# Matmuls of zeros ahead of the first load, of the coarse scores and of the local transposes

## The chip, the cores and the metric

The kernel runs on one core of one Trainium2 chip. The metric is device time in microseconds (us) of one execution. The median of 3 runs of the kernel before is 862.72 us (860.76 to 865.24).

## What is computed

Attention on q, k, v of shape (4, 8, 576, 64) in float32, and two gated layers on its output. The attention has two parts that are added: a coarse one on means of 4 neighbours, repeated 4 times, and a local one in which each position sees the positions less than 4 away.

```python
q_d, k_d, v_d = (x.reshape(B, H, S // 4, 4, D).mean(axis=3) for x in (q, k, v))
out_up = np.repeat(sm_attn(q_d, k_d, v_d), 4, axis=2)
mask = np.abs(pos[:, None] - pos[None, :]) < 4
scores = np.where(mask, scale * q @ k.T, -1e9)
out_local = softmax(scores) @ v
x = (out_up + out_local)           # to 2304 tokens x 512
x = max(x @ w1, x @ w2, x @ w3) @ w_out
out = ((x @ w_a) * (x @ w_b)) @ w_out2
```

## The kernel before

The work has three stages. The attention runs over 16 items, each a batch and a pair of heads. The first layer follows in six blocks of 384 tokens, and the second layer in products that TensorE runs almost without a gap. The matrices of both layers are split into a high and a low part, and every product is three matmuls. The weights come in as 8-byte numbers and are converted on VectorE in four steps (`convert_steps`, lines 519 to 536: `ce`, `cm`), then split by ScalarE (line 541) and GpSimd (line 542).

An item goes through six steps. `a_load_qk` and `a_load_v` (letters k and v) issue its loads on SP's queue: q, k, the coarse v (`vr`, line 230) and the windows of v (`vw`, line 254). `a_qk` (Q) transposes q and k on TensorE for the first eight items (`ps_t`, lines 291 and 296), copies them out on ScalarE (`kt`, `qt`) and sums them on VectorE to coarse ones (`kd`, `qp`, scaled into `qd`). `a_scores` (S) runs the coarse scores (`ps_sd`, line 322), the mask (`ps_s`, line 327: a bf16 matmul of 320 columns) and the local scores (line 340), and the two softmaxes: maxima `md` and `ml`, exponentials `ed` and `el`, sums, and on GpSimd the division of `ed` (line 383) and of `el` (line 390). `a_tr` (T) adds up the coarse v on GpSimd (`vr`, line 401, in place; `vd`, line 402) and transposes `ed` (`ps_td`, line 412) and `el` (`ps_tl`, line 423). `a_av` (A) runs the weighted sums (`ps_ud`, line 438; `ps_av`, line 460), adds them on VectorE (`x`, line 470) and splits the result (`xh` on ScalarE, `xl` on GpSimd, line 484).

The strings `PRE` and `LOOPS` say in which order the steps of several items are written: at item i the loads are two or three items ahead, the transposes of q and k two ahead, and the scores one ahead. From item 4 on, pieces of the first layer (`ps_m`, line 654) are mixed in at a lower priority. Within the attention the engines' orders aren't those of the text: a scheduler puts instructions in order by a timeline of its own, so an added instruction can move others on every engine. At run time each engine and each queue keeps its order and waits at the head of it. After the attention the order is that of the text (`manual_schedule`).

PSUM gives the attention eight banks: `bk("t")` and `bk("v")` take three in turn, and all other names five in turn. The items below 8 with an odd number share one `vr` tile, and all the others share another, so a new `vr` load waits until GpSimd has read the old one (`vd`).

Of the kernel before, what the change touches and what calls it, by code (L numbers as in the profile page):

```python
# [10 lines left out]
BF16 = mybir.dt.bfloat16  # L11
# [34 lines left out]
SUM_ACT = (0, 1, 2, 3, 4, 6, 7, 8, 9, 10, 13, 14, 15)  # L46
NORM_POOL = (0, 1, 2, 3, 4, 5, 6, 7, 8, 9, 10, 11, 13, 14, 15)
ADD_PSUM = range(16)


@with_exitstack
def attn_moe_kernel(
# [14 lines left out]
    nc = tc.nc  # L67
# [4 lines left out]
    P = 128  # L72
# [4 lines left out]
    TB = 384  # L77
# [5 lines left out]
    RF = S // P  # L83
    RT = S - RF * P
# [12 lines left out]
    def win(t):  # L97
        return t * QT - (FAC - 1)

    def clip(t):  # L100
        return max(win(t), 0), min(win(t) + KW, S)

    def nq(t):
        return min(QT, S - t * QT)
# [12 lines left out]
    def bk(st, name):  # L117
        if 1 in psp_:
            return psp_[1].tile([P, 512], F32, tag="m", name=name)
        t, n = ("t", 3) if st in "tv" else ("m", 5)  # L120
        return psp_[0].tile([P, 512], F32, tag=t, name=name, bufs=n)
# [3 lines left out]
    ap_ = attn_ctx.enter_context(tc.tile_pool(name="attn", bufs=1, side="right"))  # L125
# [4 lines left out]
    def at(v):  # L130

        return tc.high_priority(offset=tc.cur_priority - int(v))

    ident = cst.tile([P, P], F32, name="ident")
    make_identity(nc, ident)
# [48 lines left out]
    def pool(i, n):  # L184

        return ex if i < NI // 2 and i % n == n - 1 else ap_
# [9 lines left out]
    TV = NI // 2  # L196
# [114 lines left out]
    def half_of(j, t):  # L311

        return 1 - j if t >= NP2 else j
# [3 lines left out]
    def a_scores(i):  # L317
        s = st[i]
        psd = bk("s", "ps_sd")
        pd = psd[: 2 * DQ, : NDQ * SD].rearrange("m (t k) -> m t k", t=NDQ)  # L320
        for t in range(NDQ):
            nc.tensor.matmul(  # L322
                pd[:, t, :], s["qd"][:, t].rearrange("m j i -> m (j i)"), s["kd"], start=True, stop=True
            )
        psl = [bk("s", "ps_s") for _ in GS]
        for (g0, g1), ps in zip(GS, psl):
            nc.tensor.matmul(
                ps[:, : (g1 - g0) * KW],
                identb,
                cap[:, g0:g1, :].rearrange("m t k -> m (t k)"),  # L330
                start=True,
                stop=True,
            )
        for j, t in order_s:
            half = half_of(j, t)
            g = int(t >= GS[1][0])
            pj = slice(64 * j, 64 * j + 64)
            k0, k1 = clip(t)
            o = (t - GS[g][0]) * KW - win(t)
            nc.tensor.matmul(  # L340
                psl[g][64 * half : 64 * half + nq(t), o + k0 : o + k1],
                s["qt"][pj, t * QT : t * QT + nq(t)],
                s["kt"][pj, k0:k1],
                start=False,
                stop=True,
                skip_group_check=True,
            )
        ed = s["ed"] = pool(i, 3).tile([2 * DQ, NDQ, SD], F32, tag="ed", bufs=1 if pool(i, 3) is ex else 2, name="ed")
        el = s["el"] = pool(i, 3).tile([P, NQ, KW], F32, tag="el", bufs=1 if pool(i, 3) is ex else 2, name="el")
        md = pool(i, 3).tile([2 * DQ, NDQ, 1], F32, tag="md", bufs=1 if pool(i, 3) is ex else 2, name="md")  # L350
        sd = pool(i, 3).tile([2 * DQ, NDQ, 1], F32, tag="sd", bufs=1 if pool(i, 3) is ex else 2, name="sd")
        ml = pool(i, 3).tile([P, NQ, 1], F32, tag="ml", bufs=1 if pool(i, 3) is ex else 2, name="ml")
        sums = epss[i % 3]
        sl = pool(i, 3).tile([P, NQ, 1], F32, tag="sl", bufs=1 if pool(i, 3) is ex else 2, name="sl")
        if i in SUM_ACT:
            nc.vector.tensor_reduce(out=md[:, :, 0], in_=pd, axis=AX.X, op=ALU.max, negate=True)
            for t in range(NDQ):
                nc.scalar.activation(
                    out=ed[:, t, :],
                    in_=pd[:, t, :],  # L360
                    func=AF.Exp,
                    bias=md[:, t, :],
                    accum_out=sums[: 2 * DQ, NQ + t, :1],
                )
        else:
            nc.vector.tensor_reduce(out=md[:, :, 0], in_=pd, axis=AX.X, op=ALU.max)
            nc.vector.tensor_tensor(out=ed, in0=pd, in1=md.to_broadcast([2 * DQ, NDQ, SD]), op=ALU.subtract)
            nc.scalar.activation(out=ed, in_=ed, func=AF.Exp)
        for (g0, g1), ps in zip(GS, psl):
            e = el[:, int(g0 > 0) :: 2, :]  # L370
            n = g1 - g0
            p3 = ps[:, : n * KW].rearrange("m (t k) -> m t k", t=n)
            nc.vector.tensor_reduce(out=ml[:, g0:g1, 0], in_=p3, axis=AX.X, op=ALU.max)
            nc.vector.tensor_tensor(
                out=e, in0=p3, in1=ml[:, g0:g1, :].to_broadcast([P, n, KW]), op=ALU.subtract
            )
            nc.scalar.activation(out=e, in_=e, func=AF.Exp, scale=SCALE)
        if i not in SUM_ACT:
            nc.vector.tensor_reduce(out=sums[: 2 * DQ, NQ:, 0], in_=ed, axis=AX.X, op=ALU.add)
        nc.vector.tensor_reduce(out=sd[:, :, 0], in_=sums[: 2 * DQ, NQ:], axis=AX.X, op=ALU.add)  # L380
        nc.vector.reciprocal(sd, sd)
        eng = nc.gpsimd if i in NORM_POOL else nc.vector
        eng.tensor_tensor(out=ed, in0=ed, in1=sd.to_broadcast([2 * DQ, NDQ, SD]), op=ALU.mult)
        for g0, g1 in GS:
            e = el[:, int(g0 > 0) :: 2, :]
            n = g1 - g0
            nc.vector.tensor_reduce(out=sums[:, g0:g1, 0], in_=e, axis=AX.X, op=ALU.add)
            nc.vector.tensor_reduce(out=sl[:, g0:g1, 0], in_=sums[:, g0:g1], axis=AX.X, op=ALU.add)
            nc.vector.reciprocal(sl[:, g0:g1], sl[:, g0:g1])
            nc.gpsimd.tensor_tensor(  # L390
                out=e, in0=e, in1=sl[:, g0:g1, :].to_broadcast([P, n, KW]), op=ALU.mult
            )
# [4 lines left out]
    def a_tr(i):  # L397
        s = st[i]
        s["vd"] = ap_.tile([DK, NDK, 2, D], F32, tag="vd", bufs=2, name="vd")
        vr = s["vr"].rearrange("p h c f d -> p (h c) f d")  # L400
        nc.gpsimd.tensor_tensor(out=vr[:, :, 0:2, :], in0=vr[:, :, 0:2, :], in1=vr[:, :, 2:4, :], op=ALU.add)  # L401
        nc.gpsimd.tensor_tensor(
            out=s["vd"].rearrange("p c h d -> p h c d"),
            in0=s["vr"][:, :, :, 0, :],
            in1=s["vr"][:, :, :, 1, :],
            op=ALU.add,
        )
        ptd = s["ptd"] = pool(i, 2).tile([DK, NDK, NDQ * 2 * DQ], F32, tag="ptd", bufs=1, name="ptd")
        for c in range(NDK):
            ps = bk("t", "ps_td")  # L410
            for t in range(NDQ):
                nc.tensor.transpose(
                    ps[:DK, t * 2 * DQ : (t + 1) * 2 * DQ],
                    s["ed"][:, t, c * DK : (c + 1) * DK],
                    ident[: 2 * DQ, : 2 * DQ],
                )
            nc.scalar.copy(ptd[:, c, :], ps[:DK, : NDQ * 2 * DQ])
        pt = s["pt"] = []
        for u0 in range(0, NP2, TG):
            ps = bk("t", "ps_tl")  # L420
            n = min(TG, NP2 - u0)
            for u in range(n):
                nc.tensor.transpose(  # L423
                    ps[:, u * P : (u + 1) * P],
                    s["el"][:, 2 * (u0 + u) : 2 * (u0 + u) + 2, :].rearrange("m a x -> m (a x)"),
                    ident,
                )
            x = pool(i, 2).tile([P, TG, P], F32, tag="pt", bufs=3, name="pt")
            nc.scalar.copy(x[:, :n].rearrange("m t k -> m (t k)"), ps[:, : n * P])
            pt.append(x)  # L430

    def a_av(i):
# [34 lines left out]
        for (g0, g1), ps in zip(AVG, pss):  # L467
            a0, a1 = g0 * QT, min(g1 * QT, S)
            if i in ADD_PSUM:
                mark['d', i] = nc.vector.tensor_tensor(  # L470
# [5 lines left out]
            else:  # L476
                nc.scalar.copy(x32[:, a0:a1], ps[:, : a1 - a0])
        if i not in ADD_PSUM:
            xg = x32.rearrange("m (g f) -> m g f", f=FH)
# [582 lines left out]
    for x in PRE.split():  # L1062
        if x == "w":
            w_prefetch()
        elif x == "s":
            with at(tc.cur_priority + 0):
                w_step(1)
        else:
            emit(x[0], int(x[1:]))
# [208 lines left out]
```

## Time and profile before

| | us |
|---|---|
| Median of 3 runs | 862.72 |
| The profiled execution, its own time | 866.62 |
| Its span, first to last instruction | 864.8 |
| TensorE (PE) busy | 831.2 |
| VectorE (DVE) busy | 625.9 |
| GpSimd (POOL) busy | 368.8 |
| ScalarE (ACT) busy | 336.3 |

The span is the time that the trace shows; 1.8 us of the execution lie outside it. PE's busy time is that of its matmuls, whose ends are modelled, and it doesn't tell a matmul at 2.4 GHz from one at 1.2 GHz; the granted clock of a stretch (1.00 or 0.50 of full speed) does. The profiled execution is 3.9 us (0.45%) slower than the median.

### The profile page before, as it was taken

What the parts mean: (1) busy time and instruction counts of PE and PEld (TensorE: products, weight loads), DVE (VectorE), ACT (ScalarE), POOL (GpSimd) and SP (SyncE); (2) the same over time, 40 slices, a digit from 0 to 9 for tenths busy, and PEclk for the clock granted to TensorE, in tenths of its full rate; (3) what the DMA queues carried; (4) which work ended last, traced back from release to release, by engine and by line L of the source; (5) the groups of instructions that cost most, each with busy time, mean ns of one, the idle gap of its engine ahead of it and who ended that gap; (6) DMA issues with size and microseconds to landing.
All of it is one profiled execution on the core that took longest, in us unless ns stands there. A gap on an engine that the chain in (4) does not pass through costs nothing.

```text
span 864.8 us, 14914 instructions
## 1 busy us (share of the span) xinstructions
PE 831.2 (96%) x5686; PEld 771.1 (89%) x5686; DVE 625.9 (72%) x1110; ACT 336.3 (39%) x755; POOL 368.8 (43%) x354
## 2 busy tenths in 40 slices
PE   5988989999999999999989999999999999999998
PEld 3667778899999999999988999999999799999997
DVE  5989987765664795696788899999999754234344
ACT  4775645543321231332435553443444332322211
POOL 3865775442322241334546654645554341111111
PEclk9799899999999999999999999999999999999999
DMA  8896764411220130231324454544453268666612
GB/s 182 181 180 140 146 122 96 78 29 31 72 73 25 51 96 25 90 142 73 110 98 147 171 185 156 183 181 161 181 183 134 99 223 303 231 216 219 243 49 74
DMA packets 125553, 116.32 MB, mean 135 GB/s; under 512 B 81834, under 2 KB 108202, under 8 KB 125482
## 3 DMA queue, kind: packets, MB, share of 16 engines
q1 hardware_dynamic: 121306, 98.59, 38.3%
q10 hardware_dynamic: 4176, 16.78, 5.5%
q8 instruction: 45, 0.74, 0.4%
q14 instruction: 26, 0.21, 0.1%
HBM read 80.74 MB, written 34.60 MB: 133 GB/s over the span
## 4 chain that ended last, share of the span: by engine, by line
PE 74%; DVE 10%; DMA 6%; POOL 5%; issue 3%; ACT 1%; SPq 1%; DVEq 0%; POOLq 0%; ACTq 0%
PE ps_m L654 45%; PE ps_u L911 23%; DMA vr<-in_v_dram 4%; PE ps_av L460 1%; DVE ce L519 1%; POOL el L390 1%; PE ps_tl L423 1%; POOL vr L401 1%; DVE ce L529 1%; PE ps_ud L438 1%; DVE g L940 1%; PE ps_sd L322 1%; DMA w<-y 1%; DVE cm L522 1%; PE ps_s L340 1%
## 5 line engine op out<-in xcount | busy, mean ns | idle before, releaser
L654 PE MATMUL ps_m<-xh,w 128*128 128x384 f32 x864 | 174.5, 340 | 0.3 <-ACT xh L483 0.3
L950 POOL TENSOR_TENSOR gl<-g,gh 128x384 fp32r<-128x384 f32 x72 | 78.0, 1083 | 185.6 <-ACT gh L949 156.2
L654 PEld LDWEIGHTS ps_m<-xh,w 128*128 128x128 f32 x864 | 152.4, 190 | 2.3 <-issue 0.8
L911 PE MATMUL ps_u<-xh,w 128*128 128x384 f32 x720 | 135.9, 338 | 0.1
L911 PEld LDWEIGHTS ps_u<-xh,w 128*128 128x128 f32 x720 | 128.1, 190 | 2.7 <-DVE t L683 0.4
L654 PE MATMUL ps_m<-wo,gh 128*128 128x512 f32 (+1 forms) x422 | 126.9, 393 | 1.5 <-DVE acc L1019 1.3
L911 PE MATMUL ps_u<-xl,w 128*128 128x384 f32 x648 | 122.2, 336 | 1.6 <-ACT sn L923 1.6
L911 PEld LDWEIGHTS ps_u<-xl,w 128*128 128x128 f32 x648 | 113.7, 188 | 5.0 <-ACT sn L923 2.5
L654 PE MATMUL ps_m<-xl,w 128*128 128x384 f32 x432 | 94.3, 336 | 1.7 <-POOL xl L484 1.7
L923 ACT COPY sn<-ps_u 128x384 f32<-128x384 f32 x108 | 50.6, 479 | 113.2 <-PE ps_u L911 99.4
L683 DVE TENSOR_TENSOR t<-ps_m,t 128x384 f32<-128x384 f32 x72 | 39.9, 554 | 72.7 <-PE ps_m L654 65.2
L654 PEld LDWEIGHTS ps_m<-wo,gh 128*128 128x128 f32 x422 | 78.0, 188 | 15.4 <-DVE acc L1019 3.0
L1019 DVE TENSOR_TENSOR acc<-ps_m,acc 128x512 f32<-128x512 f32 (+1 forms) x91 | 61.2, 679 | 41.6 <-PE ps_m L654 41.6
L654 PEld LDWEIGHTS ps_m<-xl,w 128*128 128x128 f32 x432 | 76.3, 188 | 2.1 <-POOL xl L484 1.9
L654 PE MATMUL ps_m<-hh,wo 128*128 128x384 f32 x288 | 74.0, 336 | 2.4 <-DVE acc L710 2.4
L689 POOL TENSOR_TENSOR hl<-t,hh 128x384 fp32r<-128x384 f32 x36 | 37.0, 1026 | 69.3 <-ACT hh L688 68.2
L654 PE MATMUL ps_m<-wo,gl 128*128 128x512 f32 x211 | 66.2, 392 | 0.0
L949 ACT CAST gh<-g 128x384 fp32r<-128x384 f32 x72 | 37.1, 515 | 71.4 <-DVE g L940 67.7
L710 DVE TENSOR_TENSOR acc<-ps_m,acc 128x384 f32<-128x384 f32 x120 | 61.7, 552 | 0.6 <-PE ps_m L654 0.5
L526 ACT ACTIVATE ce<-ce,ebias 128x512 int16<-128x512 uint16 x60 | 43.3, 722 | 45.4 <-DVE ce L519 45.3
L842 POOL TENSOR_TENSOR w<-F,w 128x768 fp32r<-128x768 f32 (+1 forms) x36 | 56.6, 1589 | 5.2 <-ACT w L840 4.6
L527 DVE SCALAR_TENSOR_TENSOR cm<-raw,cm 128x512 f32<-128x512 uint32 x60 | 56.3, 938 | 1.5
(131 smaller groups left out, 1334.7 us busy)
## 6 DMA issues: line engine op xcount, KB each, us to landing
dw<-w SPq DMA_DIRECT2D x24, 768.0 KB
raw<-in_moe_w_dram SPq DMA_DIRECT2D x18, 512.0 KB
raw<-in_moe_w_out_dram SPq DMA_DIRECT2D x18, 512.0 KB
w<-dw SPq DMA_DIRECT2D x12, 768.0 KB
w<-dw ACTq DMA_DIRECT2D x12, 768.0 KB
dw<-wo SPq DMA_DIRECT2D x12, 512.0 KB
wo<-dw ACTq DMA_DIRECT2D x11, 512.0 KB
vw<-in_v_dram SPq DMA_DIRECT2D x62, 80.0 KB
```

The source lines that it names most:

```text
L526: nc.scalar.activation(out=s16, in_=e, func=AF.Relu, bias=ebias, scale=8.0)
L527: nc.vector.scalar_tensor_tensor(out=f, in0=lo, scalar=2.0**-32, in1=m, op0=ALU.mult, op1=ALU.add)
L654: nc.tensor.matmul(ps, lhs[a], rhs[b], start=(i == 0), stop=(i == n - 1))
L683: nc.vector.tensor_tensor(out=t, in0=ps, in1=cur["t"], op=ALU.max)
L689: nc.gpsimd.tensor_tensor(out=l, in0=t, in1=h.bitcast(F32), op=ALU.subtract)
L710: nc.vector.tensor_tensor(out=a, in0=ps, in1=a, op=ALU.add)
L842: nc.gpsimd.tensor_tensor(out=l, in0=w, in1=h.bitcast(F32), op=ALU.subtract)
L911: nc.tensor.matmul(ps, w[:, a, slot, kk], y[:, b * HK + kk], start=start and i == 0, stop=i == 3 * HK - 1, skip_group_check=not start,)
L923: nc.scalar.copy(t, ps)
L949: nc.scalar.copy(h, g)
L950: nc.gpsimd.tensor_tensor(out=l, in0=g, in1=h.bitcast(F32), op=ALU.subtract)
L1019: nc.vector.tensor_tensor(out=a, in0=ps, in1=a, op=ALU.add)
```

## The change

A tile `idle` of zeros, 128 x 384 in bf16, is written once by VectorE. A helper `warm` runs a given number of matmuls of it into a PSUM bank: 128 x 128 zeros as weights, 384 columns. Nothing reads the results. It stands in three places: 14 matmuls ahead of everything that TensorE does; for items 0 to 8 in the bank of the coarse scores ahead of these scores (9, 9, 4, 4, 4, 4, 4, 4, 3), for items 0 to 7 behind one more transpose of the tail of q; and for items 0 to 9 in the bank of the local transposes ahead of these (8, 4, 4, 4, 4, 4, 4, 4, 6, 6). That is 14 + 45 + 48 = 107 matmuls, each with its load of weights, and 8 transposes.

```diff
+WARM_FIRST = 14
+WARM_S = (9, 9, 4, 4, 4, 4, 4, 4, 3)
+WARM_T = (8, 4, 4, 4, 4, 4, 4, 4, 6, 6)
...
+    idle = ap_.tile([P, TB], BF16, name="idle")
+    nc.vector.memset(idle, 0.0)
+
+    def warm(ps, n):
+
+        for _ in range(n):
+            nc.tensor.matmul(ps[:, :TB], idle[:, :P], idle, start=True, stop=True)
+
+    warm(bk("q", "ps_w"), WARM_FIRST)
+
     ident = cst.tile([P, P], F32, name="ident")
...
         psd = bk("s", "ps_sd")
+        if i < len(WARM_S):
+            if i < TV:
+                nc.tensor.transpose(psd[:, :RT], s["q"][:RT, RF], ident[:RT, :RT])
+            warm(psd, WARM_S[i])
         pd = psd[: 2 * DQ, : NDQ * SD].rearrange("m (t k) -> m t k", t=NDQ)
...
             ps = bk("t", "ps_tl")
+            if u0 == 0 and i < len(WARM_T):
+                warm(ps, WARM_T[i])
             n = min(TG, NP2 - u0)
```

Line numbers behind the added code grow by 4 to 20. On GpSimd, between the setup and the third weight piece, this stood before (`ed` of items 0 and 1, `el` of items 0 and 1, the coarse v of item 1, then 0, then 2 and 3):

```order
L383 TENSOR_TENSOR ed<-ed,sd 96x432
L401 TENSOR_TENSOR vr<-vr 72x4x128
L542 TENSOR_TENSOR w_141<-cm,w_140 128x512
L390 TENSOR_TENSOR el<-el,sl 128x5x64
L401 TENSOR_TENSOR vr<-vr 72x4x128
L390 TENSOR_TENSOR el<-el,sl 128x5x64
L402 TENSOR_TENSOR vd<-vr 72x2x2x64 x2
L383 TENSOR_TENSOR ed<-ed,sd 96x432
L542 TENSOR_TENSOR w_141<-cm,w_140 128x512
L390 TENSOR_TENSOR el<-el,sl 128x5x64 x2
```

On the same engine, from the same place on, this stands there now:

```order
L419 TENSOR_TENSOR vr<-vr 72x4x128
L401 TENSOR_TENSOR ed<-ed,sd 96x432
L562 TENSOR_TENSOR w_158<-cm,w_157 128x512
L408 TENSOR_TENSOR el<-el,sl 128x5x64 x2
L419 TENSOR_TENSOR vr<-vr 72x4x128
L420 TENSOR_TENSOR vd<-vr 72x2x2x64 x2
L562 TENSOR_TENSOR w_158<-cm,w_157 128x512
L401 TENSOR_TENSOR ed<-ed,sd 96x432
L408 TENSOR_TENSOR el<-el,sl 128x5x64
L419 TENSOR_TENSOR vr<-vr 72x4x128
L504 TENSOR_TENSOR xl<-x_446,xh 128x384
L504 TENSOR_TENSOR xl<-x_446,xh 128x192
```

Both halves of item 0's `el` (line 390, now 408) have moved ahead of the second wait for a `vr` load, and the second half of item 1's `el`, which stood ahead of `xl` and of the `vr` of items 2 and 3, now comes behind them (it is the next row but two).

On SP's queue, between the `vr` load of item 7 and that of item 8 (the first and the last row), this stood before:

```order
L230 DMA vr<-in_v_dram 72x4x256
L254 DMA vw<-in_v_dram 64x5x64 x4
L505 DMA raw<-in_moe_w_dram 128x4x256
L210 DMA k<-in_k_dram 32x18x32 x4
L210 DMA q<-in_q_dram 32x18x32
L254 DMA vw<-in_v_dram 64x5x64 x4
L210 DMA q<-in_q_dram 32x18x32 x3
L230 DMA vr<-in_v_dram 72x4x256
```

And this stands on SP's queue now, from the `vr` load of item 7 on:

```order
L244 DMA vr<-in_v_dram 72x4x256
L525 DMA raw<-in_moe_w_dram 128x4x256
L224 DMA q<-in_q_dram 32x18x32 x4
L244 DMA vr<-in_v_dram 72x4x256
L268 DMA vw<-in_v_dram 64x5x64 x4
L525 DMA raw<-in_moe_w_out_dram 128x1024
L224 DMA k<-in_k_dram 32x18x32 x4
```

Between the `vr` loads of items 7 and 8 stood 17 issues, and now 5 stand there.

On PE, ahead of the last of item 9's weighted sums, 133 matmuls of the first layer (`ps_m`) stood before, and 130 stand there now.

## Rows read from the trace of the kernel before

**Rows 1.** Busy time by stretch: us, engines' busy us (instructions), PE clock, DMA share, GB/s

```profile
0.00:131.30 131.30, 108.63 (x1334) 87.36 (x1335) 111.20 (x257) 78.40 (x236) 86.38 (x109) 0.88 0.77 156
131.30:864.80 733.50, 722.61 (x4353) 683.71 (x4353) 514.72 (x853) 257.85 (x519) 282.44 (x246) 1.00 0.38 131
```

**Rows 2.** Waits of PE, 0 to 131.3 us: us in total, times, longest

```profile
PE ps_tl L423 <- POOL el L390: 8.4, 5, 3.1
PE ps_t L291 <- DMA k<-in_k_dram: 3.9, 1, 3.9
PE ps_sd L322 <- ACT qd L265: 3.5, 2, 1.8
```

**Rows 3.** PE alone in seven stretches: busy us (x), clock, DMA share, GB/s

```profile
3.86:14.20 10.34, 7.55 (x65) 1.00 0.84 193
...
28.17:34.98 6.81, 6.81 (x66) 0.51 0.76 185
...
sum 41.03, PE 36.07; mean PE 5.15
```

**Rows 4.** Timeline of PE: start, us, operation, count, idle before and its releaser

```profile
3.86 1.09 PE L291 MATMUL ps_t<-ident,k 128*128 128x128 f32 x4 [3.86 <-DMA k<-in_k_dram]
...
10.78 0.74 PE L327 MATMUL ps_s<-cap,identb 128*128 128x320 bf16 x2
...
16.54 0.60 PE L291 MATMUL ps_t<-ident,k 128*128 128x128 f32 x4
...
22.62 0.47 PE L327 MATMUL ps_s<-cap,identb 128*128 128x320 bf16 x1
...
65.47 0.43 PE L327 MATMUL ps_s<-cap,identb 128*128 128x320 bf16 x2
```

**Rows 5.** Waits of DVE, 0 to 131.3 us

```profile
DVE qp L302 <- PE ps_t L291: 6.7, 3, 4.9
DVE md L356 <- PE ps_sd L322: 2.7, 2, 2.3
```

**Rows 6.** All engines, 20 to 120 us; then 67.64 to 71.14 us

```profile
20.00:120.00 100.00, 86.48 (x1106) 68.79 (x1107) 94.74 (x218) 65.48 (x202) 71.26 (x76) 0.86 0.77 157
...
67.64:71.14 3.50, 2.73 (x24) 2.14 (x18) 3.50 (x3) 2.09 (x9) 3.50 (x6) 1.00 0.67 147
```

**Rows 7.** Line 527 in 20 to 120 us (busy, mean ns); then all (min/median/max ns)

```profile
L527 DVE SCALAR_TENSOR_TENSOR cm<-raw,cm 128x512 f32<-128x512 uint32 x7 | 10.2, 1456 | 0.0
...
L527 DVE SCALAR_TENSOR_TENSOR cm<-raw,cm x60: 641/693/3503, 13.6 to 670.5; 128x512 f32<-128x512 uint32 x60
```

**Rows 8.** Timeline of POOL, and its wait for `vr` to 131.3 us

```profile
26.05 1.17 POOL L390 TENSOR_TENSOR el<-el,sl 128x320 f32<-128x320 f32 x1
27.18 1.86 POOL L402 TENSOR_TENSOR vd<-vr 72x256 f32<-72x256 f32 x2
...
31.65 1.40 POOL L390 TENSOR_TENSOR el<-el,sl 128x320 f32<-128x320 f32 x2
...
35.73 2.93 POOL L401 TENSOR_TENSOR vr<-vr 72x512 f32<-72x512 f32 x2
...
74.19 0.72 POOL L402 TENSOR_TENSOR vd<-vr 72x256 f32<-72x256 f32 x1
...
86.00 1.27 POOL L401 TENSOR_TENSOR vr<-vr 72x512 f32<-72x512 f32 x1 [6.15 <-DMA vr<-in_v_dram]
...
POOL vr L401 <- DMA vr<-in_v_dram: 24.7, 9, 6.2
```

**Rows 9.** Timeline of SP's queue: issue of `vr` of items 2 and 3, and of 8

```profile
30.52 0.88 SPq L230 DMA_DIRECT2D vr<-in_v_dram  x2
...
82.29 0.41 SPq L230 DMA_DIRECT2D vr<-in_v_dram  x1
```

**Rows 10.** Timeline of PE: local transposes of items 0 and 1

```profile
27.27 0.76 PE L423 MATMUL ps_tl<-ident,el 128*128 128x128 f32 x5 [1.86 <-POOL el L390]
...
36.95 0.55 PE L423 MATMUL ps_tl<-ident,el 128*128 128x128 f32 x3
```

## The prediction

> **What bounds the kernel now.** I read the busy time by stretch first, because the change touches ten items at the front alone. Up to 131.3 us, where item 9's weighted sums end, PE is busy 108.6 us and idle 22.7; behind that point it is busy 722.6 of 733.5 us [rows 1]. So what is behind 131.3 us is bound by PE and stays as it is, and a lead or a lag at that point is handed on almost whole. How much of the first layer is mixed in by then hardly changes either, as the order stands: 133 of its matmuls before, 130 now.
>
> Ahead of that point I read who waits. PE waits 8.4 us for GpSimd's `el` ahead of the local transposes, 3.9 us for the first load, and 3.5 us for ScalarE's `qd` ahead of the coarse scores [rows 2]. These are the places where the zeros stand. Then the clock: six stretches granted near half speed, and the first one, whose record says 1.00 but whose transposes take 1.09 us for four against 0.60 later, hold 36.1 us of PE's work [rows 3, 4]. The falls come behind waits of PE, as the stretch that begins at 28.17 us comes behind the wait of 1.86 us that ended at 27.27 [rows 3, 10].
>
> Last, the other engines. VectorE is busy 94.7 us of the 100 between 20 and 120 us [rows 6], more than PE. GpSimd waits 24.7 us for the loads of `vr`, and what stands behind such a wait in its order is late with it [rows 8].
>
> **What is added, and its price.** The nearest row to an idle matmul is the mask's: bf16, 128 x 128 weights, 320 columns. At half clock two of them take 0.74 us and one 0.47, so one follows another in 0.27; at full clock the two take 0.43 [rows 4]. By columns (384 to 320) an idle matmul costs 0.32 us at 1.2 GHz, and I take half of that, 0.16, at 2.4 GHz; both are estimates. The 107 cost 17.2 us at full clock and 34.2 at half. The first 14 will be at half, which adds 2.2. The eight transposes are narrower than those of k at 0.60 us for four, so they cost 1.2 us at most, and I take that. The one memset on VectorE, and the loads of weights beside the matmuls, I cost at nothing: at its place VectorE waits for PE, the longest time 4.9 us [rows 5], and if that cover were gone the memset would cost no more than some tenths, by `vd`'s 0.72 us for a longer operation on GpSimd [rows 8].
>
> **What the clock gives back.** If no stretch falls to half speed, 36.1 us of work become 18.0. So PE's own account to 131.3 us is 108.6 + 17.2 + 2.2 + 1.2 - 18.0 = 111.2 us, 2.6 more than now. The zeros cost what the clock returns. A gain can come only out of the 22.7 us in which PE is idle: 131.3 - 111.2 = 20.1 us is the bound on that side. On the other side, if the clock stays low, 93 matmuls ahead of scores and transposes cost 30.0 us, of which the waits of 8.4 and 3.5 us take 11.9: 18 us slower. Between these ends the chain of waits decides, so I walk it.
>
> **The start.** The 14 matmuls wait for the memset alone. No row shows how early VectorE can run it; with 1 us as an estimate and 4.5 for the matmuls, they end 1.6 us behind the first load's 3.86 [rows 4]. Against that, transposes at full clock save 0.5 us for each four. I take 0 here, with 1.6 lost and 1.0 gained as its ends.
>
> **Item 0.** Both halves of its `el` now stand ahead of GpSimd's second wait for `vr`; the second half ended at 27.2 us [rows 8], and PE's local transposes followed at 27.27 [rows 10]. Its `vd` moves up by that half, 1.2 us, and the half-speed transposes of k behind it lose another 0.5. With the smaller shares of the sums I take 2.0 us gained.
>
> **Item 1.** Here the new order is worse. Its `el` ran at 31.65 us; its second half now stands behind the `vr` of items 2 and 3, which were issued at 30.52 [rows 9] and read from 35.73 to 38.66, behind one `vd` and two `xl` [rows 8]. At 0.9 us for each of these three that half ends at about 35.7 + 2.9 + 2.8 + 0.7 = 42.1 us, and the transposes at 36.95 [rows 10] come some 5 us later. SP's queue repays this: the load of item 8's `vr` could have been issued when `vd` of item 6 ended at 74.9, and was issued at 82.29, behind 17 others; GpSimd waited 6.15 us for it at 86.0, with item 6's `el` behind [rows 8, 9]. With 5 between, up to 6 us of that go. The load of item 5 moves up in the same way. What is late next is VectorE.
>
> **The limit.** VectorE has 5.3 us idle between 20 and 120 us [rows 6]. A faster PE can take these, not its work. I take 4 of the 5.3. That gives 2.0 + 4.0 = 6.0 us at 131.3, handed to the end.
>
> VectorE's busy time isn't all work, though. Line 527 takes 1.46 us on average between 20 and 120 us and 0.64 at best, and 3.50 at worst, from 67.64 us on [rows 7]; in just these 3.50 us GpSimd is busy all the time [rows 6]. For its seven runs alone that is 7 x 0.82 = 5.7 us of waiting that depends on how GpSimd's work falls. In the new order it can shrink or grow, which is why I don't go to the end of the 5.3.
>
> The Trainium skill (SBUF — State Buffer, "Who interferes with whom") says that a VectorE instruction with two SBUF inputs and a GpSimd instruction that reads SBUF exclude each other, the loser blocked for the whole of the other. The trace agrees with it at 67.64 us. By that rule a GpSimd whose waits shrink gives VectorE fewer openings, so the conversions would get no shorter and the gain would end at item 0's 2.0 us: the first rival below.
>
> **Sum.** 866.6 us for the profiled execution becomes 860.6. It was 3.9 us above the median, so the median goes from 862.7 to 856.7. What a measurement tells from no change here is about 0.5%, 4.3 us: faster is below 858.4, slower above 867.0.
>
> **Rivals.**
>
> *VectorE holds the pace* (18%). The zeros run inside waits that end when they ended before, and VectorE's conversions wait for GpSimd as they do now. For it speaks 94.7 us busy of 100; against it, that VectorE waits 6.7 and 2.7 us for PE at transposes and coarse scores [rows 5]. Only part of item 0 is gained, the 5 us of item 1 are repaid and no more: 861 to 864 us. The rule of the Trainium skill (SBUF — State Buffer, "Who interferes with whom") points to this case.
>
> *Item 1's `el` is not repaid* (14%). GpSimd stands at the `vr` of items 2 and 3, PE waits 5 us ahead of item 1's transposes, and all later items are that much late; the clock falls in that wait, and a stretch such as the one of 6.81 us at half speed, all of it work [rows 3], loses 3.4 more. With 2.0 gained at item 0 that is 5 + 3.4 - 2.0 = 6.4 us: 869. It decides from the point where less than 1 us of the 5 comes back through SP's earlier loads.
>
> *Everything gives way* (18%). VectorE's waits beside GpSimd shrink with the new order by half or more of the 5.7 us of line 527 and of the like in the other conversion steps, and PE's idle time goes from 22.7 to under 12. Then 9 to 16 us are gained: 847 to 854.
>
> That the zeros don't raise the clock is part of the second rival; that they are hidden and raise it is common to the other cases.
>
> **How the numbers follow.** The forecast has 50%, its own range 853.7 to 860.7 (2 to 9 us gained). About three quarters of it lie below 858.4: 0.37 and the 0.18 of the last rival make 0.55 for faster. The rest of it and the first rival make 0.30 for no change, and the second 0.15 for slower with a margin. The range to hold 8 of 10 runs from 847, the far end of the largest gain, to 867, where the slower case begins.
>
> **What would show it.** The granted clock should be 1.00 from some 6 us on, with one or no stretch at half speed to 131 us. Idle matmuls should take 0.16 us each. PE's wait for `el` ahead of item 0's transposes should be gone, the one ahead of item 1's should be new and of 3 to 5 us. GpSimd's 6.15 us wait at 86 should shrink below 2. VectorE between 20 and 120 us should stay above 94 us busy. Item 9's sums should end near 125 us, and the rest should take 733 us as now. The prediction is wrong if that rest changes by over 3 us, if VectorE's busy time up to item 9 falls by over 6 us, or if PE's idle time there, with the zeros counted as work, stays above 18.

## The result and the profile after

The changed kernel takes 874.32 us (median of 6 runs, 870.14 to 878.54); the kernel before took 862.55 beside it (6 runs). The ratio is 1.012, 95% interval 1.0081 to 1.0158: slower by 11.8 us, where 6.0 us faster was forecast, and above the range that was given. The profiled execution took 878.54 us with a span of 876.2; it is 4.2 us above its median, as the one before was 3.9 above its own.

Busy time by stretch comes first, cut where item 9's weighted sums end (142.41 us now, 131.3 in [rows 1]), then the stretch of [rows 6] and the two longest at half clock; the columns are those of [rows 1].

```profile
0.00:142.41 142.41, 125.35 (x1444) 94.52 (x1445) 109.32 (x257) 79.44 (x235) 84.98 (x109) 0.88 0.71 144
142.41:876.25 733.84, 722.75 (x4358) 684.54 (x4358) 515.61 (x854) 257.80 (x520) 282.01 (x245) 1.00 0.38 130
20.00:120.00 100.00, 87.27 (x1084) 65.71 (x1084) 86.59 (x199) 60.11 (x180) 65.07 (x69) 0.86 0.71 149
41.00:51.00 10.00, 10.00 (x113) 7.09 (x113) 7.97 (x19) 4.66 (x17) 5.25 (x6) 0.51 0.63 163
78.00:92.00 14.00, 13.64 (x116) 9.15 (x116) 12.02 (x20) 6.83 (x19) 8.90 (x9) 0.51 0.51 109
```

The whole loss is ahead of that cut: 11.1 us of it, and behind it 733.84 us stand against 733.50. PE is busy 16.7 us longer and idle 17.1 us in place of 22.7. The granted clock is 0.88, as before: the zeros did not keep it up. VectorE is busy 86.6 us of 100 in place of 94.7 [rows 6], so it is further from full than it was.

The waits of PE to 142.41 us, and those of GpSimd, answer to [rows 2] and [rows 8]: us in total, times, longest.

```profile
PE ps_tl L443 <- POOL el L408: 7.2, 3, 3.9
PE ps_td L430 <- POOL ed L401: 2.7, 1, 2.7
PE ps_ud L458 <- POOL vd L420: 2.2, 1, 2.2
...
POOL vr L419 <- DMA vr<-in_v_dram: 33.7, 8, 11.9
POOL el L408 <- DVE sl L407: 6.3, 4, 3.4
```

The waits ahead of the first load and of `qd` are gone, as they should be: zeros run there now. But PE now waits 2.7 us for item 5's `ed` and 2.2 us for `vd`, both of GpSimd, and GpSimd stands 33.7 us at `vr`, 9 more than before (11.9 of them ahead of the first `vr`, which now comes ahead of item 0's `ed`). Where that is, the timelines of GpSimd and PE show.

```profile
34.77 1.27 POOL L419 TENSOR_TENSOR vr<-vr 72x512 f32<-72x512 f32 x1 [2.32 <-DMA vr<-in_v_dram]
...
39.86 0.90 POOL L408 TENSOR_TENSOR el<-el,sl 128x320 f32<-128x320 f32 x1
...
74.27 1.26 POOL L419 TENSOR_TENSOR vr<-vr 72x512 f32<-72x512 f32 x1 [5.62 <-DMA vr<-in_v_dram]
...
77.41 0.90 POOL L401 TENSOR_TENSOR ed<-ed,sd 96x432 f32<-96x432 f32 x1
78.27 1.39 POOL L408 TENSOR_TENSOR el<-el,sl 128x320 f32<-128x320 f32 x2
```

```profile
24.98 0.77 PE L443 MATMUL ps_tl<-ident,el 128*128 128x128 f32 x5 [0.26 <-POOL el L408]
27.95 0.72 PE L458 MATMUL ps_ud<-ptd,vd 72*64 72x144 f32 x8 [2.20 <-POOL vd L420]
...
40.82 1.32 PE L443 MATMUL ps_tl<-ident,el 128*128 128x128 f32 x5 [3.94 <-POOL el L408]
44.69 1.46 PE L144 MATMUL ps_sd<-idle 128*128 128x384 bf16 x4
...
78.36 0.70 PE L430 MATMUL ps_td<-ident,ed 96*72 96x96 f32 x3 [2.66 <-POOL ed L401]
...
80.90 1.46 PE L144 MATMUL ps_tl<-idle 128*128 128x384 bf16 x4
...
90.98 1.13 PE L480 MATMUL ps_av<-pt,vw 64*64 64x58 f32 x40
...
114.96 0.77 PE L443 MATMUL ps_tl<-ident,el 128*128 128x128 f32 x5 [3.02 <-POOL el L408]
```

Item 5's sums in the kernel before:

```profile
82.47 0.80 PE L460 MATMUL ps_av<-pt,vw 64*64 64x58 f32 x40
```

Item 1's `el` is behind the `vr` of items 2 and 3, as foreseen, and PE waits 3.94 us. At item 5 the same happens again: its `ed` and `el` now stand behind the `vr` of item 7, which GpSimd awaited for 5.62 us. Behind both waits the clock is at half (the stretches from 41 and from 78 us above), and four zeros then take 1.46 us ahead of work that is ready. Item 4's sums end 0.9 us later than they did; item 5's begin at 90.98 us in place of 82.47, and from there to item 9 the lag stays at 8 to 13 us.

### The profile page after: what moved, and what is told of

The parts are those of the page before. It is cut to its first block, busy times and chain, and to the rows that moved or that the text cites. A ratio compares the mean times of both kernels' runs of the same rounds, so it can differ in the third digit from the quotient of the medians.

```text
span 876.2 us, 15160 instructions
## 1 busy us (share of the span) xinstructions
PE 848.1 (97%) x5801; PEld 779.1 (89%) x5801; DVE 624.9 (71%) x1111; ACT 337.2 (38%) x755; POOL 367.0 (42%) x354
## 4 chain that ended last, share of the span: by engine, by line
PE 83%; DVE 6%; DMA 4%; POOL 3%; issue 2%; SPq 2%; ACT 1%; DVEq 0%; POOLq 0%; ACTq 0%
PE ps_m L674 48%; PE ps_u L931 26%; DMA vr<-in_v_dram 3%; PE ps_s L358 1%; PE ps_av L480 1%; PE ps_ud L458 1%; PE ps_tl L443 1%; PE ps_sd L340 1%; PE ps_td L430 1%; SPq L232 1%; PE ps_tl L144 1%; DMA w<-y 1%; PE ps_sd L144 1%; POOL vr L419 1%; SPq L235 0%
## 5 line engine op out<-in xcount | busy, mean ns | idle before, releaser
L674 PE MATMUL ps_m<-xl,w 128*128 128x384 f32 x432 | 94.7, 337 | 0.0
L549 DVE SCALAR_TENSOR_TENSOR ce<-raw,ce 128x512 uint16<-128x512 uint16 x60 | 45.5, 758 | 16.2 <-ACT ce L546 16.1
```

Of the source, the lines that this page charges most:

```text
L549: nc.vector.scalar_tensor_tensor(out=e, in0=top, scalar=0x8000, in1=e, op0=ALU.bitwise_and, op1=ALU.bitwise_or)
L674: nc.tensor.matmul(ps, lhs[a], rhs[b], start=(i == 0), stop=(i == n - 1))
```

## The experiments

The change does three things at once: it adds zeros, it adds eight transposes that read q, and it lets the scheduler put every engine in another order. To tell them apart, most kernels here are **pinned**: a table holds, for each engine, the order in which the built program of the kernel before (the **old** order) or of the changed kernel (the **new** order) has its instructions, and each instruction is tied behind the one ahead of it by an edge that orders issue and waits for nothing. In the old order each group of zeros stands right ahead of the coarse scores or local transposes that it belongs to.

```diff
+PINNED = {
+    "PE": "0-44 80-85 45-58 60 63-64 67-68 71-72 75-76 ...
...
+    pin()
     ctx.enter_context(tc.manual_schedule())
```

Inside `pin()`, `row` is an engine's list in the table's order:

```python
for prev, ins in zip(row, row[1:]):
    tc.add_manual_dep(
        ins,
        prev.name,
        mybir.DependencyInfo(mybir.DependencyClass.NoSync, mybir.DependencyReason.DATA),
        reason="order",
    )
```

Ratios are to the kernel before, with their 95% intervals. The kernel before was measured anew beside each group of runs (medians of 862.55 to 865.15 us), so it is the ratios that can be compared, not the medians. Where the intervals of two kernels overlap, a difference between the two is at best likely.

| kernel | order | extra transposes | zeros | median, us | ratio |
|---|---|---|---|---|---|
| changed kernel | new | of q | 384 columns | 874.32 | 1.012 (1.0081 to 1.0158) |
| zeros_old | old | of q | 384 | 872.49 | 1.0106 (1.0072 to 1.0141) |
| thin_new | new | of q | 16 | 872.40 | 1.0114 (1.0082 to 1.0146) |
| thin_old | old | of q | 16 | 870.65 | 1.0097 (1.006 to 1.0135) |
| hold_only | old | of q | none | 868.59 | 1.0042 (1.0018 to 1.0066) |
| zeros_nohold_old | old | none | 384 | 865.11 | 1.0009 (0.9989 to 1.003) |
| thin_nohold_old | old | none | 16 | 867.22 | 1.0011 (0.9985 to 1.0038) |
| nohold_new | new | of the identity | 384 | 871.25 | 1.0068 (1.0043 to 1.0092) |
| thin_nohold_new | new | of the identity | 16 | 875.36 | 1.0114 (1.0085 to 1.0143) |
| first_old | old | none | first 14 only | 862.69 | 0.9994 (0.9968 to 1.0021) |

### Order, or TensorE's time?

**zeros_old** and **thin_old** are the changed kernel with the old order pinned, **thin_new** with the new one; the thin ones shorten each zero:

```diff
-            nc.tensor.matmul(ps[:, :TB], idle[:, :P], idle, start=True, stop=True)
+            nc.tensor.matmul(ps[:, :16], idle[:, :P], idle[:, :16], start=True, stop=True)
```

> All 107 zero matmuls and the 8 extra transposes run, but every other instruction keeps, on all engines, the order of the kernel before; the zeros stand right ahead of the first load's transposes, of each item's coarse scores and of its local transposes. Theory 'order' (the loss is the new order on GpSimd and SP: item 1's and item 5's division stand behind loads of vr for later items): the loss goes, 857 to 866 us, item 9's sums end at 127 to 134 us, and PE doesn't wait for ed of item 5. Theory 'TensorE time' (the zeros stand ahead of work that is ready, and the clock falls anyhow): still 870 to 878, sums at 140 us or later, with PE busy over 122 us up to there.

> The order of the changed kernel on all engines, instruction by instruction, zeros included, but each zero matmul has 16 columns in place of 384, so that it takes almost no time. Theory 'order': it stays slow, 868 to 876 us, with PE's waits of 3.9 us ahead of item 1's local transposes and of 2.7 us ahead of item 5's transposes still there. Theory 'TensorE time': back to 858 to 866.

> The order of the kernel before, with zero matmuls of 16 columns and the 8 extra transposes. Both theories: 860 to 867 us, since neither the order nor TensorE's time changes; the transposes and small matmuls cost at most 3 us. It is the fourth corner: zeros_old against it is the price of the zeros' time under the old order, thin_new against it the price of the new order without that time.

**first_old** has `WARM_S = ()` and `WARM_T = ()`, pinned to the old order.

> Only the 14 zero matmuls ahead of the first load, the order of the kernel before. Both theories: 859 to 866 us. The transposes of items 0 and 1 at full clock save up to 1 us each; if the clock then stays full to 28 us, item 0's weighted sums at 30.2 us come 1 to 3 us earlier; what is left of that at item 9's sums (131.3 us) shows whether a lead at the front is handed on.

Neither theory held. thin_new stays slow, as "order" had it, but zeros_old stays slow too, as "TensorE time" had it; and thin_old, where both expected 860 to 867, took 870.65. What all four slow kernels share is the eight transposes. The start is worth nothing, as forecast: in first_old item 0's sums begin at 30.77 us (30.24 before). At 0.9994 first_old also shows that the pinning itself costs nothing that can be seen.

### The transposes hold q

A transpose of q's tail in `a_scores` reads q one step later than `a_qk` did. Items share two q buffers, so the load of a later q waits for it, at the head of SP's queue.

**hold_only** keeps the transposes and leaves all zeros out; **zeros_nohold_old** keeps the zeros and leaves the transposes out, both in the old order:

```diff
-                nc.tensor.transpose(psd[:, :RT], s["q"][:RT, RF], ident[:RT, :RT])
```

> No zero matmul at all: the order of the kernel before, with only the 8 extra transposes of q's tail ahead of the coarse scores of items 0 to 7. New theory 'hold': such a transpose reads q again one step later than the kernel before did, so q's buffer comes free later, and SP's queue stands at the next load of q (SP waited 5.4 and 3.5 us for these transposes with all zeros in the old order, 3.9 and 1.8 us in the changed kernel) with all loads behind it: 868 to 874 us, the loss whole. Theory 'zeros' (the zeros themselves cost it, even at 16 columns, by their loads of weights and the banks that they write): 861 to 866.

> All 107 zero matmuls at full size, the order of the kernel before, without the 8 extra transposes. 'Hold': 855 to 865 us, and SP's queue doesn't wait for ps_sd. 'Zeros': 869 to 875, as with them.

**nohold_new** (new order, pinned) and **nohold_free** (left to the scheduler) transpose the identity in place of q:

```diff
-                nc.tensor.transpose(psd[:, :RT], s["q"][:RT, RF], ident[:RT, :RT])
+                nc.tensor.transpose(psd[:, :RT], ident[:RT], ident[:RT, :RT])
```

> The changed kernel, its order kept on every engine instruction by instruction, but the 8 extra transposes read the identity in place of q: the same work on TensorE, and q's buffer comes free as before. 'Hold': 858 to 867 us; what it stays above zeros_nohold_old is the price of the new order. 'Order': 870 to 876, as the changed kernel. 'Zeros': 870 to 876.

> The changed kernel with the 8 extra transposes on the identity, and the scheduler free to order it anew (it does: 48 of GpSimd's and 67 of SP's rows move). 'Hold': 855 to 866 us, by the luck of the new order. 'Zeros': 868 to 876. It can't tell 'order' from 'hold' by itself.

hold_only shows a part of the loss and not the whole: 868.59 us, ratio 1.0042, with its profiled execution (span 871.0) at the slow end of its runs. It shows the mechanism with nothing else in the way. First SP's queue (its waits for these transposes up to item 9's sums, then what it issued), then PE and GpSimd, and last what the DMA moved in 20 to 62 us, in 40 equal slices:

```profile
SPq L238 <- PE ps_sd L342: 5.5, 3, 3.7
...
29.91 0.61 SPq L241 DMA_DIRECT2D k<-in_k_dram  x1
34.27 0.37 SPq L238 DMA_DIRECT2D q<-in_q_dram  x1
34.74 2.41 SPq L250 DMA_DIRECT2D vr<-in_v_dram  x2
```

```profile
33.93 0.31 PE L342 MATMUL ps_sd<-ident,q 64*128 64x64 f32 x1
...
42.95 0.63 PE L311 MATMUL ps_t<-ident,q 128*128 128x128 f32 x4 [3.10 <-DMA q<-in_q_dram]
```

```profile
40.78 1.26 POOL L424 TENSOR_TENSOR vr<-vr 72x512 f32<-72x512 f32 x1 [4.18 <-DMA vr<-in_v_dram]
```

```profile
GB/s 167 224 249 169 169 156 119 105 202 121 181 16 0 8 99 46 46 211 206 187 261 263 201 195 153 115 210 87 274 348 254 146 157 153 138 138 68 246 213 188
```

Item 2's extra transpose runs at 33.93 us, behind item 0's sums. SP, done with k at 30.52, issues the q of item 4, which goes into the same buffer, only at 34.27; for some 3 us the DMA moves next to nothing (16, 0 and 8 GB/s). The `vr` of items 2 and 3, behind it in the queue, go out at 34.74 where they went at 30.52 [rows 9], and GpSimd reads the first at 40.78 in place of 35.73 [rows 8]. PE then waits 3.10 us for that q.

zeros_nohold_old is at 1.0009: without the transposes the zeros cost nothing that can be seen in the old order. So there the hold is a cause: with it 1.0106 and, at 16 columns, 1.0097; without it 1.0009 and, in thin_nohold_old below, 1.0011. Why it costs 0.4% alone and 1.0% beside zeros was not found.

In the new order the loss goes only from 1.012 to 1.0068, with intervals that overlap, and nohold_free is at 1.0058 (1.0036 to 1.008). So the new order is a cause by itself, and what the hold adds to it is not shown. SP's queue waits 5.7 us for such transposes in the changed kernel too, but it has the `vr` of items 2 and 3 ahead of that q and issues them at 30.08 us (30.52 before), so these weren't held:

```profile
30.08 2.03 SPq L244 DMA_DIRECT2D vr<-in_v_dram  x2
...
35.35 1.62 SPq L232 DMA_DIRECT2D q<-in_q_dram  x2
```

### What in the new order?

**fix17** is nohold_new with GpSimd's two places of the first section put back; **fix17_hold** is the changed kernel with the same. In GpSimd's table (one row a line, `a` and `b` the halves of `el`):

```diff
 el1b
+el1a
 vr2
 xl0 xl1 vr3 vd2
-el1a
...
-vr7
 w63 vd6 ed5 el5b el5a
+vr7
```

> nohold_new (full zeros, extra transposes on the identity, the changed kernel's order) with two moves on GpSimd alone: the first load-bound step of item 7's vr goes behind the divisions of item 5 (ed, both halves of el), and both halves of item 1's el go ahead of item 2's vr, as in the kernel before. If the price of the new order sits in these two places, item 1's and item 5's transposes come some 3 and 7 us earlier and the time falls from 871 to 863 to 867 us (item 9's sums end at 131 to 134 us in place of 137.1). If it sits in the new order of the other engines, it stays at 869 to 873.

> The changed kernel itself, the transposes of q's tail included, with only these two moves on GpSimd. 'Hold': SP's queue still stands at the transposes of q, so most of the loss stays: 869 to 874 us. 'Order' (these two places are the loss): 862 to 867.

fix17 took 872.0 us (1.0102, 1.0074 to 1.0129), fix17_hold 869.94 (1.0066, 1.0041 to 1.009). Item 5's sums did come at 81.38 us in fix17, 6 us earlier than in nohold_new; item 6's came at 100.22, against 102.86, and item 9's ended at 133.21, against 137.12. So more than half of what was put right at item 5 was lost again one item later. The 3.9 us at item 9 are between the fastest of fix17's six runs and the slowest of nohold_new's, for these were the ones profiled; the medians and ratios show no gain. fix17_hold lies below the changed kernel (1.012), with intervals that touch. My reading of the first section, that these two places are the loss, found no support.

**thin_nohold_new**, **thin_nohold_old** (thin zeros in nohold_new and zeros_nohold_old) and **sp_old** (nohold_new with SP alone in the old order) came next, with **double_old** for the section below:

> nohold_new (the changed kernel's order on every engine, extra transposes on the identity) with zeros of 16 columns. If the new order by itself costs the 5 us that nohold_new lies above zeros_nohold_old, it stays at 868 to 873 us. If the zeros cost it, because the new order puts them ahead of work that is ready, it falls to 861 to 866.

> zeros_nohold_old with zeros of 16 columns: the old order, no extra transposes, almost no time of TensorE, and a clock that falls as in the kernel before. 861 to 866 us if the held q is what made thin_old slow (870.65); 868 to 873 if the many short matmuls with their loads of weights did.

> nohold_new, but SP's queue issues its loads in the order of the kernel before; the four other engines keep the changed kernel's order, zeros at full size. If the new order of the loads is the price, 861 to 867 us; if the order of the engines is, 868 to 874, or more, as the two orders no longer fit each other.

thin_nohold_new is at 1.0114: the new order costs 1.1% by itself, without the hold and without time for zeros. It is also where thin_new is with the hold, 1.0114. Three pairs of the new order thus differ by the hold alone, and with it they are at +0.5% (changed kernel and nohold_new), 0.0 (the thin ones) and -0.4 (fix17_hold and fix17): taken together, no effect that can be told from none. With the identity the zeros at full size come to 1.0068, under the 1.0114 of the thin ones; with q they don't (1.012 and 1.0114), so it isn't shown that the clock that they return is worth something here. thin_nohold_old at 1.0011 clears the short matmuls. sp_old took 890.94 us (1.0302, 1.0273 to 1.0332): SP's old order under the others' new one is far worse, so the loads can't be taken by themselves.

Last, two kernels whose work had been measured in the old order were left to the scheduler: **first_free** (the work of first_old) and **zeros_nohold_free** (that of zeros_nohold_old).

> The work of first_old (only the 14 zeros ahead of the first load), but the scheduler orders it anew: 39 of 350 rows of GpSimd and 43 of SP's 356 move. first_old was 0.9994 of the kernel before, so what this lies above it is the price of an order alone. If any order that the scheduler makes anew is worse than the one the kernel before was tuned to: 866 to 874 us (0.3 to 1.1 per cent above). If the changed kernel's order was a rare bad one: 861 to 865.

> The work of zeros_nohold_old (all zeros, no extra transposes), ordered anew: 74 rows of GpSimd and 94 of SP move. zeros_nohold_old was 1.0009. A new order costs: 867 to 876 us. A rare bad order in the changed kernel: 861 to 866, and this would be the version to keep.

first_free took 860.57 us (0.9951, 0.9932 to 0.997), which is below both kernels of this study; zeros_nohold_free took 866.08 (1.0023, 1.0007 to 1.0039). The same work in another order thus moved by -0.4 and +0.1% in these two (the second not clear of none), and by +0.6 and +1.0% in nohold_new and thin_nohold_new (but for their eight transposes of the identity, which no run has in the old order). Which rows of an order make it good was not found: the profiled executions of first_free and first_old have spans of 860.4 and 860.0 us.

### Why does a full clock gain nothing?

zeros_nohold_old has what the change was to bring: here to item 9's sums, between 20 and 120 us, and between 32.4 and 100.

```profile
0.00:131.71 131.71, 117.10 (x1441) 90.00 (x1441) 112.21 (x258) 78.02 (x236) 87.25 (x109) 0.95 0.80 156
...
20.00:120.00 100.00, 91.69 (x1186) 70.59 (x1185) 95.63 (x219) 65.33 (x204) 72.36 (x75) 0.95 0.81 157
32.40:100.00 67.60, 61.62 (x870) 46.58 (x869) 65.67 (x153) 43.88 (x138) 48.89 (x50) 1.00 0.83 162
```

The granted clock is 0.95 (0.88 before), and 1.00 for 68 us on end. PE's idle time falls from 22.7 to 14.6 us, its busy time grows from 108.6 to 117.1, and the sums end at 131.71 us: 131.3 before. VectorE is busy 95.6 of the 100 us.

**double_old** doubles `WARM_S` and `WARM_T` in it.

> zeros_nohold_old with twice the zeros ahead of the coarse scores and the local transposes: 93 more, by 0.16 us each 15 us more of TensorE's time. If TensorE has slack at the front, as its 14.6 us of idle time there say, most of it is hidden: 864 to 870 us. If each zero stands on the path, so that the first 93 were paid for by the clock alone, it costs 10 to 15 us: 874 to 880.

It took 869.27 us (1.0056, 1.0039 to 1.0074), 0.47% or 4 us more than zeros_nohold_old: of some 15 us of zeros about 11 lie in waits. PE is then full between 20 and 120 us:

```profile
0.00:135.80 135.80, 129.23 (x1534) 97.59 (x1534) 105.15 (x258) 78.23 (x236) 88.30 (x109) 0.96 0.76 152
...
20.00:120.00 100.00, 98.43 (x1225) 73.92 (x1225) 85.73 (x212) 63.37 (x194) 69.71 (x71) 0.96 0.76 151
```

**light_before** and **light_zeros** are the kernel before and zeros_nohold_old, old order, with two conversion steps of the eight weight pieces in the attention on 128 of 512 columns:

```diff
-        nc.vector.scalar_tensor_tensor(out=f, in0=lo, scalar=2.0**-32, in1=m, op0=ALU.mult, op1=ALU.add)
+        nc.vector.scalar_tensor_tensor(
+            out=f[:, :n], in0=lo[:, :n], scalar=2.0**-32, in1=m[:, :n], op0=ALU.mult, op1=ALU.add
+        )
...
+        if n < NP_:
+            out, i0, i1 = (x[:, :n] for x in (out, i0, i1))
```

> The kernel before, its order kept, with two of the four conversion steps of the eight weight pieces in the attention (the ones that write cm from raw and cm from ce) on 128 of 512 columns: it leaves out three quarters of that work, about 12 us of VectorE up to item 9. If VectorE sets the pace of the front, the time falls by 4 to 12 us, to 851 to 860; if TensorE and its clock do, it stays within 3 us of the kernel before.

> zeros_nohold_old (all zeros, the old order, no extra transposes) with the same work of VectorE left out. If VectorE's pace is what hid the gain of the full clock, it now shows: 3 to 8 us below light_before. If the zeros cost as much of TensorE's time as the clock returns, it is within 2 us of light_before, or above it.

light_before took 861.74 us (0.9986, 0.9963 to 1.0009), light_zeros 863.56 (0.9995, 0.9974 to 1.0015): no sure gain for either, and the zeros gain nothing here too. But VectorE was lightened less than meant: in light_before its busy time to item 9's sums fell by 6.6 us (111.2 to 104.6), not 12, since the two steps kept 0.7 and 0.8 of their mean time with a quarter of the columns. (Its profiled execution, 3.6 us under its median, ended these sums at 125.8 us; the ratio shows no such gain.) Line 537 of light_before is the row of [rows 7] with a quarter of the columns, grouped between 20 and 120 us:

```profile
L537 DVE SCALAR_TENSOR_TENSOR cm<-raw,cm 128x128 f32<-128x128 uint32 x7 | 7.0, 1007 | 0.0
```

So this pair doesn't settle whether VectorE sets the pace. What is shown is that TensorE's time is not most of it: with the clock at 0.95 and 8 us of its idle time gone the end stays, and 15 us more of its work, at the same clock, move the end by 4. If the first 93 zeros cost those 4 us too, the full clock was worth about as much and they ate it up; that is an estimate from double_old, and no run has the clock without the zeros.

## Why the prediction was wrong

Two steps failed: the walk of the new order, at "SP's queue repays this", and the price of the eight transposes, 1.2 us at most. The runs showed in their place that the new order costs 0.6 to 1.0% without the transposes of q, and that these cost 0.4 to 1.0% in the old order. The signs that the prediction gave for itself being wrong did not see it: the rest moved by 0.3 us, VectorE's busy time to item 9's sums fell by 1.9, and PE's idle time was 17.1, where 3, 6 and 18 were the limits.

**The bound and the rest** were right: 733.84 us behind item 9's sums, 733.50 before, and the lag there was handed to the end whole. In the profiles of the experiments that rest takes 729.4 to 734.2 us, so the end of item 9's sums tells differences between kernels only to some 4 us.

**The price of a zero** was right: 0.16 us at full clock and 0.32 at half; four take 0.81 us at 34.87 and 1.46 at 44.69 (with their tails), the first 14 take 4.66 us. All 107 hold PE for 26.4 us in the changed kernel and 24.4 in zeros_nohold_old, tails included, where 17.2 + 2.2 were counted.

**"The eight transposes ... cost 1.2 us at most"** failed. They were priced as work of PE. Their price is that they read q: 0.4% alone, 1.0% with zeros beside them, in the old order. The text said that zeros stand "behind one more transpose of the tail of q", and never asked who waits for that tail. In the changed kernel itself, with its new order, no run shows this price.

**"What the clock gives back"** held only as a condition. In the changed kernel four stretches at half speed remain behind the start: one from 17 us, behind waits for ScalarE, and three behind the waits for GpSimd that end at 40.82, 78.36 and 114.96. PE was busy 125.4 us where 111.2 was worked out. That alone isn't the loss, though: thin_new, whose zeros take almost no time, has PE busy for 119.16 us, ends item 9's sums at 138.05 and is as slow.

```profile
0.00:138.05 138.05, 119.16 (x1444) 94.59 (x1445) 107.26 (x257) 78.45 (x235) 86.72 (x109) 0.81 0.72 149
```

In zeros_nohold_old nearly all of the clock came back, and PE's account was 117.1 us: 5.9 us more than the forecast had it; the nine zeros ahead of item 1's scores still ran at half there (3.04 us).

**Item 0** gained 1.1 us, not 2.0: its local transposes came 2.3 us earlier (24.98 us), and then its coarse sums waited 2.20 us for `vd`. **Item 1** was right as to its wait, 3.94 us and new, which ended at 40.82 us, and so was SP: the load of item 8's `vr` was issued at 77.47 us and GpSimd took it without a wait, where it had waited 6.15 us [rows 8]. Item 1's sums ended 8 us later than before, but by item 3 the lag was repaid (its sums ended at 65.1 us, as before).

**"SP's queue repays this"** failed behind that. Only the places that had waits in the trace of before were walked in the new order. At item 5, where before had none, `ed` and `el` stood behind item 7's `vr`. This is the step that failed in the changed kernel: its end is late by the order as a whole, 1.1% in thin_nohold_new and 0.7 in nohold_new. Item 5's place shows in the trace, but to put it and item 1's right brought no gain of the median in fix17, so which places carry the loss is open.

**"The limit"** failed for the changed kernel: VectorE was busy 86.6 us, not over 94, and the 4.0 us that were to be taken from its idle time did not come. The first rival, that the zeros run inside waits that end when they ended before, fits the old order without the transposes, at 1.0009; whether VectorE is what holds that pace stays open. The second rival had the sign and a part of the mechanism, not its places.

**What stays open**: why the new order costs 1.1% and that of first_free returns 0.4%; whether the held q adds to the loss in the new order; and what sets the pace of the front where TensorE doesn't. SP's queue is a candidate, since 3 to 4 us of it lost at 30 us in hold_only were not made up.

## What to carry to other kernels

An added instruction is priced by what it reads as well as by its time: ask which buffer it holds longer, which load waits for that buffer, and what is queued behind that load. Where a scheduler makes the order, pin the old order before judging an edit, since the same work in another order moved here by -0.4 to +1.0%, as much as the whole edit did in the old order (1.1%) and far more than its zeros did (0.1%). Ask also whether a cause that is shown in one order holds in another: the held q cost 1% in the old order here, and nothing that could be seen in the new one. Before adding filler work that is to keep the clock up, look whether TensorE sets the pace, for filling its idle time was no gain by itself here.

## What was not expected of the hardware

How long a VectorE step takes can depend on GpSimd more than on its size. Line 527 took 1456 ns on average for 512 columns [rows 7], and for 128 columns 1007 in light_before and 680 in light_zeros. Two of these short ones, and what GpSimd did at the time:

```profile
65.69 3.25 DVE L537 SCALAR_TENSOR_TENSOR cm<-raw,cm 128x128 f32<-128x128 uint32 x1
...
82.14 0.24 DVE L537 SCALAR_TENSOR_TENSOR cm<-raw,cm 128x128 f32<-128x128 uint32 x1
```

```profile
64.61 1.27 POOL L411 TENSOR_TENSOR vr<-vr 72x512 f32<-72x512 f32 x1 [2.89 <-DMA vr<-in_v_dram]
65.83 0.74 POOL L412 TENSOR_TENSOR vd<-vr 72x256 f32<-72x256 f32 x1
66.52 0.92 POOL L393 TENSOR_TENSOR ed<-ed,sd 96x432 f32<-96x432 f32 x1
67.39 1.41 POOL L400 TENSOR_TENSOR el<-el,sl 128x320 f32<-128x320 f32 x2
...
83.65 1.27 POOL L411 TENSOR_TENSOR vr<-vr 72x512 f32<-72x512 f32 x1 [6.25 <-DMA vr<-in_v_dram]
```

At 82.14 GpSimd waits for a load, and the step takes 0.24 us; at 65.69 GpSimd is still in its `vr` and then runs four instructions back to back, and the step takes 3.25 us and ends 0.1 us behind them. The Trainium skill (SBUF — State Buffer, "Who interferes with whom") says that a VectorE instruction with two SBUF inputs contends with a GpSimd instruction that reads SBUF, that their shared ports are an exclusive lock, and that the order of issue decides who blocks. The trace agrees, and shows more: the step was held through all that stood behind the `vr`, four in a row.

With SP's queue stopped for 3.75 us in hold_only, the DMA was near idle within 2, at 0 to 16 GB/s where it had moved 105 to 249: at that place it had no backlog to live on.
